# Routed attention with a gated MLP: batch 0 in three rounds of queries, and cluster codes turned several tiles at a time

## The chip, the cores and the metric

The kernel runs on one core of one Trainium2 chip. The metric is the device time of one execution in microseconds. A core has five engines that run their own instruction streams in order and meet only by semaphores: TensorE (PE in the profile, its weight loads PEld), VectorE (DVE), ScalarE (ACT), GpSimd (POOL) and SyncE (SP), which issues most transfers.

## The reference

Four batches of eight heads, 768 positions, 64 features. Each query and each key is assigned to one of 16 centroids of its head; a query attends only to keys of its own cluster. The result, with the heads side by side, goes through an MLP of width 2048 with a SiLU gate.

```python
q_n = q / (np.linalg.norm(q, axis=-1, keepdims=True) + 1e-06)
k_n = k / (np.linalg.norm(k, axis=-1, keepdims=True) + 1e-06)
c_n = centroids / (np.linalg.norm(centroids, axis=-1, keepdims=True) + 1e-06)
q_assign = np.argmax(np.einsum('bhsd,hcd->bhsc', q_n, c_n), axis=-1)
k_assign = np.argmax(np.einsum('bhsd,hcd->bhsc', k_n, c_n), axis=-1)
mask = q_assign[:, :, :, None] == k_assign[:, :, None, :]
scores = np.where(mask, scale * np.matmul(q, k.transpose(0, 1, 3, 2)), -1000000000.0)
attn = np.exp(scores - np.max(scores, axis=-1, keepdims=True))
attn = attn / (np.sum(attn, axis=-1, keepdims=True) + 1e-09)
x = np.matmul(attn, v).transpose(0, 2, 1, 3).reshape(B * S, H * D)
h = x @ w_in
out = (h * (1.0 / (1.0 + np.exp(-h)))) @ w_out
```

## The kernel before

**Tiles.** A sequence of 768 positions is six tiles of 128. Heads are prepared in pairs (p = 0 to 3). Matmuls take float16, and the mask is made part of the scores: the operand tile "ab" holds 64 rows of features and, in rows 64 to 79, a one-hot code of the cluster, scaled so that keys of another cluster are pushed far down before the exponential.

**Preparing a pair** (`part`, from L474). A float32 tile of queries or keys is split into a high float16 half (`hi`, L524 to L531, on ACT, DVE or POOL) and the rest (`lo`, L533 to L535, on DVE), side by side in "hl". Both halves are turned so that features lie on partitions. The logits against the centroids (L615 and L619, or L624) give the cluster; `peak` and `mark` make the one-hot code on DVE.

- Batch 0 turns on TensorE against an identity (L570). It turns each tile twice: first all 128 columns of high and low half into "lt", for the logits (the settle from PSUM is L585 on ACT, L587 on DVE), and after the code is known the 80 columns of high half and code together, into "ab" (settled by L581 on ACT or L583 on DVE, where "gain" scales the code's rows). The lists `TK`, `TQ`, `TR`, `TS` choose the settling engine.
- Batches 1 to 3 turn by a transposing DMA from SP (L550). POOL subtracts the maximum (L673), DVE makes the code (L700, L702) and flips it in blocks of 32 (L715), and four copies of 16 partitions place it in "ab" (L732 on POOL, L728 by a DMA); `PUTB` gives the engine of each, here POOL, POOL, SP, POOL.

**Attention** (from L762). For each head: scores (L801, six key tiles against 256 or 512 query columns), the exponential on ACT (L808, always 512 columns), PV (L829, with a 65th column that sums the row), reciprocal and normalization on DVE (L842, L847). After each pair x is turned into "xt", by TensorE (L877, settled by L882 or L884) or by a transposing DMA (L866).

**Rounds.** Batch 0 runs its heads twice, `ROUNDS = [(0, 2), (2, 6)]`: first with the first two query tiles, then with the other four. Its MLP runs in three units of two tiles (256 columns), the other batches' in two units of three (384 columns).

**MLP** (from L896). For each of 16 blocks of width: four accumulating matmuls (L907), tanh on ACT (L913), the gate on DVE (L918); then the second matrix (L942), an eviction (L955, L957) and a store from SP. Both weights are cast to float16 on their way in by DMAs from POOL (L976, L980), each behind a one-element copy (L974) that holds it back until a chosen exponential is done.

**Order.** Nothing is run in the order in which it is written. Each step gets an engine, a planned duration, its predecessors, its buffers and a key; `Plan.order` (L88) simulates the engines and transfers in Python and always takes the step that can start first, ties by key. The instruction streams are what it puts out. `AT` and `ML` are the keys of attention and MLP; `LEADS`, `REST`, `RLOAD` and `SOON` say how far ahead a preparation is allowed to start, `sizes` how many buffers each tile has, and a filler (L353) puts matmuls of zeros into PE's planned gaps up to a planned time of `UNREAD` ns.

**Start.** The centroids' square sum, root (`c_root` on POOL, L433), reciprocal and split (L436 to L439), one transpose (L446) and four copies (L451 to L458) give "stk".

## Time and profile before

| | |
|---|---|
| three runs | 307.46, 308.21, 309.07 us; median 308.21 |
| profiled execution | 307.14 us on the device, of which the profile's span is 305.3 |
| granted TensorE clock | 0.998 of full speed |
| moved by DMA | 41.82 MB |
| code placements L732, L728 | 72 on POOL, 24 by DMA |
| first up-projection (L907) starts | 34.9 us |

The profile shows one execution. A group's line gives source line, engine, operation, output and input tile, shape and count; then the busy time in us and the mean of one in ns; then the idle time in front of it and what ended it. In a table of stages each row is a stretch of the span with its length, the busy time of each engine, the granted clock, the share of the DMA engines and GB/s. Matmuls are pipelined and their ends are modelled, so the mean of one (219 ns for a transpose) is its passage, not the pace at which they follow each other.

### The profile page before, as it was taken

The page shows a single profiled execution, that of the slowest core. Times are in us where ns is not written, and L with a number is a line of the kernel's source. Part 1 is how long each engine was busy: PE and PEld are TensorE (multiplying, and loading weights), DVE is VectorE, ACT ScalarE, POOL GpSimd, SP SyncE. Part 2 cuts the span into 40 slices and gives each one's busy share as a digit, 9 for nine tenths or more (in the row PEclk, how much of TensorE's full clock was granted, in tenths as well). Part 3 has the DMA queues.
Part 4 walks back from the last instruction along what each step waited for, and adds up shares of the span by engine and source line. Part 5 has one row for each costly group of instructions (what it writes and reads, how often), then busy time and mean ns, then how long its engine had stood idle before and what let it go on. Part 6 is the DMA issues. An engine that isn't in the chain of part 4 may idle for free.

```text
span 305.3 us, 8425 instructions
## 1 busy us (share of the span) xinstructions
PE 297.3 (97%) x3257; PEld 196.1 (64%) x3257; DVE 207.9 (68%) x493; ACT 223.7 (73%) x461; POOL 108.2 (35%) x218
## 2 busy tenths in 40 slices
PE   8999999999999999999999998999999999999995
PEld 6898777577677746666656765665655565554644
DVE  5999688778869955989766997867562323750820
ACT  5869999888988838999777998778782380642721
POOL 2546432656466480717564563733000000000000
PEclk9999999999999999999999999999999999999999
DMA  7999969993969888486969848472010201002001
GB/s 245 290 249 251 206 104 224 103 248 87 226 100 237 191 167 196 138 156 162 237 149 223 155 154 169 131 129 66 0 37 36 84 12 71 35 0 73 32 34 69
DMA packets 73688, 41.82 MB, mean 137 GB/s; under 512 B 53041, under 2 KB 70705, under 8 KB 73649
## 3 DMA queue, kind: packets, MB, share of 16 engines
q1 hardware_dynamic: 68944, 36.94, 51.4%
q0 software_dynamic: 4288, 4.20, 8.6%
q8 instruction: 25, 0.41, 0.6%
q10 hardware_dynamic: 416, 0.16, 0.2%
q14 instruction: 15, 0.11, 0.1%
HBM read 27.30 MB, written 6.29 MB: 110 GB/s over the span
## 4 chain that ended last, share of the span: by engine, by line
PE 80%; DMA 7%; ACT 5%; DVE 3%; issue 1%; POOL 1%; SPq 0%; ACTq 0%; POOLq 0%
PE bank L942 27%; PE bank L907 22%; PE bank L801 16%; PE bank L829 9%; ACT P L808 4%; DMA ab<-hl 3%; PE bank L570 3%; DMA wout_s<-in_moe_w_out_dram 2%; PE bank L624 2%; DMA nk<-in_k_dram 2%; POOL hl L531 1%; PE bank L615 1%; DVE hl L535 1%; DVE gq L918 1%; PE bank L619 1%
## 5 line engine op out<-in xcount | busy, mean ns | idle before, releaser
L808 ACT ACTIVATE P<-bank 128x512 f16<-128x512 f32 x288 | 157.8, 640 | 30.8 <-PE bank L801 29.1
L942 PE MATMUL bank<-wout_s,gq 128*128 128x512 f16 (+1 forms) x400 | 97.1, 370 | 0.4 <-DMA wout_s<-in_moe_w_out_dram 0.4
L907 PE MATMUL bank<-xt,win_s 128*128 128x384 f16 (+1 forms) x576 | 95.6, 308 | 0.0
L918 DVE SCALAR_TENSOR_TENSOR gq<-tn,bank 128x384 f16<-128x384 f32 (+1 forms) x144 | 70.1, 504 | 32.4 <-ACT tn L913 28.7
L801 PE MATMUL bank<-ab 80*128 80x256 f16 (+1 forms) x384 | 90.9, 326 | 0.0
L913 ACT ACTIVATE tn<-bank 128x384 f32<-128x384 f32 (+1 forms) x144 | 67.8, 488 | 24.1 <-PE bank L907 20.9
L907 PEld LDWEIGHTS <-win_s 128*128 128x128 f16 x576 | 55.0, 97 | 28.8
L942 PEld LDWEIGHTS <-gq 128*128 128x128 f16 x400 | 37.9, 98 | 33.1 <-issue 0.7
L829 PEld LDWEIGHTS <-P 128*128 128x128 f16 x1152 | 45.6, 97 | 11.9 <-ACT P L808 0.8
L829 PE MATMUL bank<-vt,P 128*128 128x65 f16 x1152 | 49.8, 193 | 0.7 <-ACT P L808 0.6
L732 POOL COPY ab<-ohT 16x384 f16<-16x384 f16 x72 | 39.3, 546 | 28.2 <-DVE ohT L715 11.7
L801 PEld LDWEIGHTS <-ab 80*128 80x128 f16 x384 | 34.6, 97 | 20.7 <-DVE ab L583 0.2
L673 POOL TENSOR_TENSOR Df<-L,mx 128x192 f32<-128x192 f32 x24 | 12.3, 511 | 41.9 <-DVE mx L661 39.7
L957 DVE COPY ot<-bank 128x512 f32<-128x512 f32 x18 | 12.3, 681 | 16.4 <-PE bank L942 15.6
L535 DVE SCALAR_TENSOR_TENSOR hl<-nk,hl 128x384 f16<-128x384 f32 (+1 forms) x29 | 19.8, 687 | 3.3 <-POOL hl L531 3.1
L535 DVE SCALAR_TENSOR_TENSOR hl<-nq,hl 128x384 f16<-128x384 f32 (+3 forms) x33 | 20.9, 635 | 0.6 <-POOL hl L531 0.3
L641 DVE TENSOR_REDUCE L<-bank 128x192 f32<-128x384 f32 x24 | 13.3, 552 | 10.0 <-PE bank L624 9.7
L847 DVE TENSOR_TENSOR xn<-bank,rz 128x384 f16<-128x384 f32 (+2 forms) x40 | 19.1, 477 | 1.4 <-DVE rz L842 0.2
L531 POOL TENSOR_SCALAR hl<-nk 128x384 f16<-128x384 f32 (+1 forms) x25 | 13.6, 547 | 7.6 <-PE bank L570 6.7
L955 ACT COPY ot<-bank 128x512 f32<-128x512 f32 (+1 forms) x7 | 3.7, 524 | 17.2 <-PE bank L942 17.2
L531 POOL TENSOR_SCALAR hl<-nq 128x384 f16<-128x384 f32 (+2 forms) x27 | 15.2, 566 | 1.7 <-DMA nq<-in_q_dram 1.1
L417 POOL CAST vt<-nv 128x384 f16<-128x384 f32 x26 | 14.6, 582 | 1.1 <-DMA nv<-in_v_dram 0.7
(60 smaller groups left out, 183.6 us busy)
## 6 DMA issues: line engine op xcount, KB each, us to landing
nv<-in_v_dram SPq DMA_DIRECT2D x16, 384.0 KB, 5.6
out_dram<-ot SPq DMA_DIRECT2D x23, 256.0 KB, 2.3
nk<-in_k_dram SPq DMA_DIRECT2D x15, 384.0 KB, 4.3
nq<-in_q_dram SPq DMA_DIRECT2D x12, 384.0 KB, 4.7
wout_s<-in_moe_w_out_dram POOLq DMA_DIRECT2D x8, 256.0 KB, 7.2
win_s<-in_moe_w_in_dram POOLq DMA_DIRECT2D x4, 512.0 KB, 9.3
nq<-in_q_dram SPq DMA_DIRECT2D x4, 256.0 KB, 6.5
nk<-in_k_dram SPq DMA_DIRECT2D x2, 192.0 KB, 2.8
```

Of the source, the lines that this page charges most:

```text
L417: (nc.gpsimd if eng == "POOL" else nc.vector).tensor_copy(dst, src)
L531: nc.gpsimd.tensor_scalar(out=dh, in0=src, scalar1=qs, scalar2=1.0, op0=ALU.mult, op1=ALU.mult)
L535: nc.vector.scalar_tensor_tensor(out=dl, in0=src, scalar=qs, in1=dh, op0=ALU.mult, op1=ALU.subtract)
L732: nc.gpsimd.tensor_copy(dst, src)
L801: nc.tensor.matmul(banks[sb.i][:, at : at + 128 * (c1 - c0)], ab[0:80, kt[j], :], ab[0:80, qt + c0 : qt + c1, :].rearrange("p n c -> p (n ...
L808: nc.scalar.activation(out=T["P"][P.i][:, 0:at], in_=banks[sb.i][:, 0:at], func=AF.Exp, bias=0.0, scale=ESC if b else -ESC)
L829: nc.tensor.matmul(banks[O.i][:, (D + 1) * t : (D + 1) * t + nn], w, vt[:, VW * j : VW * j + nn], start=(j == 0), stop=(j == NJ - 1), skip ...
L847: nc.vector.tensor_tensor(out=T["xn"][xn.i][:, 0:nq, (h % 2) * D : (h % 2) * D + D], in0=banks[O.i][:, 0 : (D + 1) * nq].rearrange("p (t c ...
L907: nc.tensor.matmul(banks[bank.i][:, 0:n], win_s[:, r, ts(fb, 128)], T["xt"][xtb[b].i][:, r, 128 * j0 : 128 * j1], start=(r == 0), stop=(r ...
L913: nc.scalar.activation(out=T["tn"][tn.i][:, 0:n], in_=banks[bank.i][:, 0:n], func=AF.Tanh, bias=0.0, scale=1.0)
L918: nc.vector.scalar_tensor_tensor(out=T["gq"][g.i][:, fb % 4, 0:n], in0=T["tn"][tn.i][:, 0:n], scalar=1.0, in1=banks[bank.i][:, 0:n], op0=A ...
L942: nc.tensor.matmul(banks[bank.i][:, 0 : c1 - c0], T["gq"][gqs[fc // 4].i][:, fc % 4, ts(t, 128)], wout_s[:, fc, c0:c1], start=(fc == 0), s ...
```

## The change

**Rounds.** Batch 0 runs its heads three times, two query tiles each. The remaining queries are prepared in eight parts of four tiles instead of four of eight, and six of these are split wholly on POOL (`both`, in `LO` the letter P).

**Codes in batch 0.** The first turn now settles straight into "ab"; "lt" is gone. The one-hot codes go to a tile of their own, "oh", 32 columns a tile, and one transpose turns one, two or four tiles of codes at once. The pieces of 16 rows are then copied over the low half's rows in "ab" by the engines that the strings in `TQ` and `TS` name: a digit 1 or 2 gives the number of tiles turned together; without one it is four, and A, D, P or S stand for ACT, DVE, POOL or SP; POOL and SP read from an int16 copy that DVE makes.

**Others.** In batches 1 to 3, `PUTB` places the code by POOL, DVE, POOL, DVE. Two heads share a PSUM bank and one normalization where they fit. In units of 256 columns two blocks of the MLP share a bank, a tanh and a gate. The last pair of batches 1 to 3 has x turned by DMA. The centroids are turned by two transposes and placed by one copy. Buffer counts, keys, leads and engine choices are new; so are some durations and two constants in the planner. `UNREAD` goes from 80 to 60 us of planned time.

```diff
-    ROUNDS = [(0, 2), (2, 6)]
+    ROUNDS = [(0, 2), (2, 4), (4, 6)]
...
+    COUNT = [5, 4, 2, 2, 5, 8, 15, 6, 2, 2, 3, 20, 1, 3, 11, 3, 6, 7, 3, 2]
...
-    UNREAD = 80000.0
+    UNREAD = 60000.0
...
-    PUTB = ["POOL", "POOL", "SP", "POOL"]
-    VC = ["ACT", "ACT", "POOL", "ACT"]
+    PUTB = ["POOL", "DVE", "POOL", "DVE"]
+    VC = ["POOL", "ACT", "DVE", "POOL"]
...
-    TK = ["ACT", "ACT", "DVE", "DVE", "DVE"]
-    TQ = ["DVE", "ACT", "DVE", "DVE", "DVE"]
-    TR = ["ACT", "DVE", "DVE", "DVE"]
-    TS = ["ACT", "DVE", "DVE", "DVE"]
-    HI = ["ACT", "ACT", "ACT", "POOL"]
-    HR = ["DVE", "POOL", "DVE", "POOL"]
+    TK = ["DVE", "ACT", "ACT", "DVE", "ACT"]
+    TQ = ["2DA", "DDPP", "APDD", "DAAP", "DDDD"]
+    TR = ["DVE", "DVE", "ACT", "DVE", "ACT", "DVE", "ACT", "ACT"]
+    TS = ["2DD", "2DD", "DDDD", "1DA", "2DA", "2DD", "2AA", "ASDD"]
+    HI = ["ACT", "ACT", "POOL", "POOL"]
+    HR = ["ACT", "DVE", "ACT", "DVE", "DVE", "ACT", "POOL", "ACT"]
+    LO = ["P", "P", "P", "D", "P", "P", "D", "P"]
...
-    SOON = [7, 4, 7, 4]
-    XT = ["DVE", "ACT", "ACT", "DVE"]
+    SOON = [8, 9, 7, 2]
+    XT = ["DVE", "DVE", "DVE", "DVE", "DVE", "DVE", "DVE", "DVE", "DMA", "DVE", "DMA", "DMA"]
+    XL = ["DMA", "DMA", "DMA"]
...
     def c_place():
...
+        nc.vector.tensor_copy(stk.rearrange("p s h c -> p (s h c)"), banks[pc.i].bitcast(f16)[:, 0 : 2 * H * HC])
...
+            def both(views=views, qs=qs, m=m):
+                src, dh, dl = views()
+                x = T["xs"][xs.i][:, 0 : 64 * m].rearrange("p (h j d) -> p h j d", h=src.shape[1], d=D)
+                nc.gpsimd.tensor_scalar(out=x, in0=src, scalar1=qs, scalar2=1.0, op0=ALU.mult, op1=ALU.mult)
+                nc.gpsimd.tensor_copy(dh, x)
+                nc.gpsimd.tensor_tensor(out=dl, in0=x, in1=dh, op=ALU.subtract)
...
-                w = {"ACT": 200 + act_w(32 * n) * 0.75, "POOL": pool_w(32 * n), "DVE": dve_w(32 * n, 0.08, 240), "SP": 600}[code_eng[g]]
+                w = {"ACT": 200 + act_w(32 * n) * 0.75, "POOL": 155 + 32 * n, "DVE": dve_w(32 * n, 0.08, 240), "SP": 600}[code_eng[g]]
...
+                def turn_code(c0=c0, c1=c1, bk=bk):
+                    for i in range(c0, c1, side):
+                        m = min(side, c1 - i)
+                        at = (i - c0) // side * 128
+                        nc.tensor.transpose(
+                            banks[bk.i].bitcast(f16)[0 : 32 * m, at : at + 128],
+                            T["oh"][oh.i][:, i : i + m, :].rearrange("p n c -> p (n c)"), ident,
+                        )
...
+                def settle_code():
+                    nc.vector.tensor_copy(T["oc"][oc.i][:, 0:wide], banks[bank.i].bitcast(i16)[:, 0:wide])
...
+                    def put_alone(c0=c0, c1=c1, bk=bk, on_a=on_a, cols=cols, g=g):
+                        dst = T["ab"][A.i][64 : 64 + HC, a0 + c0 + g : a0 + c1 : side, :]
+                        src = banks[bk.i].bitcast(f16)[32 * g : 32 * g + HC, 0:cols].rearrange("p (n c) -> p n c", c=128)
+                        if on_a:
+                            nc.scalar.activation(out=dst, in_=src, func=AF.Copy, bias=0.0, scale=ONE)
+                        else:
+                            nc.vector.tensor_scalar(out=dst, in0=src, scalar1=ONE, scalar2=None, op0=ALU.mult)
...
+                def put_near(g=g, cols=cols):
+                    dst = T["ab"][A.i][64 : 64 + HC, a0 + g : a0 + n : 4, :]
+                    rows = slice(32 * g, 32 * g + HC)
+                    if near[g] in "PS":
+                        src = T["oc"][oc.i][rows, 0:cols].rearrange("p (n c) -> p n c", c=128)
+                        if near[g] == "P":
+                            nc.gpsimd.tensor_copy(dst, src)
+                        else:
+                            nc.sync.dma_start(dst, src)
...
+        both = 2 if 2 * nq * (D + 1) <= 512 else 1
...
-        for fb in range(NFB):
+        m = 512 // n if n >= 128 and NFB % (512 // n) == 0 and 512 // n <= 2 else 1
+        for fb in range(0, NFB, m):
...
-        return step("POOL", 840, f, after=[x], use=[use], key=-1, load=2450 if kind == "in" else 1220)
+        return step("POOL", 1180, f, after=[x], use=[use], key=-1, load=2390 if kind == "in" else 1190)
```

In `COUNT` the buffers are, in order, nk 5 (4 before), nq 4 (5), nv 2, hl 2 (3), ab 5, vt 8 (10), P 15 (18), gq 6 (7), xt 2 (3), xn 2 (3), L 3 (2), mx 20 (2), Df 1 (2), oh 3 (2), ohT 11 (3), tn 3, ot 6 (2), rz 7 (3), and the new oc 3 and xs 2.

More of the change, by code (lines that the diff above doesn't have):

```diff
@@ L47, in __init__, with step @@
         self.filler = None
-    def step(self, eng, w, fn, after=(), use=(), key=0.0, load=None, hold=0.0, pace=None, flip=False, lag=None, slack=0.0, port=False):
+    def step(self, eng, w, fn, after=(), use=(), key=0.0, load=None, hold=0.0, pace=None, flip=False, lag=None, slack=0.0, port=None):
         s = Step()
@@ L472, with part @@
     score_uses = {}
-    def part(b, p, segs, a0, due, lead=20.0, hi_eng="POOL", turn="DMA", twin=False, sub="POOL", code_eng=None, pace=None, wait=None):
+    def part(b, p, segs, a0, due, lead=20.0, hi_eng="POOL", turn="DMA", twin=False, sub="POOL", code_eng=None, pace=None, wait=None, lo_eng="D"):
         key = due - lead
@@ L576, in settle_of @@
[L576 to L584 removed]
+                            banks[bank.i].bitcast(f16)[:, (t - c0) * 128 : (t - c0) * 128 + 128],
@@ L585, in settle @@
+                            T["hl"][hl.i][:, t * 128 : t * 128 + 128], ident,
+                        )
+                def settle(bank=bank, c0=c0, c1=c1):
+                    pt = banks[bank.i].bitcast(f16)[:, 0 : (c1 - c0) * 128]
+                    out_ = T["ab"][A.i][:, a0 + c0 : a0 + c1, :].rearrange("p n c -> p (n c)")
+                    if turn[0] == "ACT":
                         nc.scalar.copy(out_, pt)
@@ L740, in part @@
         else:
-            last = {}
-            for c in chunks:
-                bank = buf("M")
-                x = step("PE", 57 * len(c), turn_of(c, bank, D, HW), after=[marks, his, s_ident], use=[hl, bank], key=key + 12 * span)
+            near = turn[1]
+            alone = near[0] in "12"
+            bank = buf("M")
+            side = int(near[0]) if alone else 4
+            wide = 128 * ((n + side - 1) // side)
+            cuts = [(c, min(n, c + 8 * side)) for c in range(0, n, 8 * side)] if alone else [(0, n)]
```

439 lines of the change are left out of this document (222 added, 217 removed).

## The prediction

> **What bounds the kernel now.** I read the page's busy line first, then the busy times by stage, then the chain of waits, then the groups by form. The first line says that TensorE (PE) is busy nearly all the time:
>
> ```profile
> PE 297.3 (97%) x3257; PEld 196.1 (64%) x3257; DVE 207.9 (68%) x493; ACT 223.7 (73%) x461; POOL 108.2 (35%) x218
> ```
>
> The stages say where it is not (columns: stage, its length, busy us of PE, weight loads, DVE, ACT, POOL with counts, granted clock, DMA share, GB/s):
>
> ```profile
> 7.60:15.00 7.40, 6.84 (x142) 6.57 (x143) 7.11 (x21) 6.56 (x12) 3.75 (x6) 1.00 1.02 299
> 15.00:20.00 5.00, 5.00 (x105) 4.54 (x103) 4.93 (x15) 4.65 (x10) 2.47 (x5) 1.00 0.97 186
> 20.00:30.00 10.00, 9.26 (x195) 8.37 (x194) 9.61 (x27) 7.80 (x17) 5.64 (x11) 1.00 1.15 278
> 30.00:50.00 20.00, 19.94 (x284) 15.46 (x281) 15.17 (x43) 19.75 (x48) 7.38 (x15) 1.00 0.94 167
> 50.00:80.00 30.00, 29.48 (x379) 20.52 (x376) 24.66 (x65) 26.98 (x60) 15.50 (x31) 1.00 0.85 157
> ...
> 120.00:160.00 40.00, 39.62 (x471) 25.62 (x470) 32.50 (x73) 35.13 (x72) 22.49 (x42) 1.00 0.72 170
> 160.00:210.00 50.00, 49.06 (x567) 31.79 (x566) 39.91 (x94) 43.15 (x87) 26.66 (x50) 1.00 0.72 152
> ```
>
> After 7.6 us PE's visible idle time is 0.56 + 0.74 + 0.06 + 0.52 + 0.38 + 0.94 = 3.2 us. Two regimes are to be seen. From 7.6 to 30 us DVE is 97% busy (21.65 of 22.4): there it sets the pace of the preparation that feeds PE. From 30 us on, MLP work is always waiting and PE itself is the bound. Matmul ends are modelled, so I tested this with the pace at which long runs issue, from the chain:
>
> ```profile
> 13.31 1.79 PE bank L570 x32
> ...
> 131.69 5.33 DMA ab<-hl
> ...
> 183.53 5.20 DMA ab<-hl
> ...
> 270.49 10.36 PE bank L942 x48
> 280.85 10.40 PE bank L907 x64
> 291.25 10.41 PE bank L942 x64
> ```
>
> These give 0.216 us for a 512-column matmul (10.36/48), 0.1625 for 384, 0.056 for a transpose (1.79/32). Times the counts (368 and 32 half ones on L942; 384, and 192 of 256 columns at 0.109, on L907; 192 + 192 on L801; 1152 at 1.09/36 = 0.030 on L829; 222 transposes; 480 logits at 0.025 to 0.03) this is about 290 us. PE's real work starts near 6.8 and ends at 301.7, so at most about 5 us of it is stall. The last 3.6 us are the last eviction and store, which nothing here touches. Thus the time is PE's work, plus about 5, plus two ends; a change pays where it removes PE instructions, or fills the ramp.
>
> **Code transposes (L570, second use).** Each of 96 tiles of batch 0 is turned twice now:
>
> ```profile
> L570 PE MATMUL bank<-ident,hl 128*128 128x128 f16 x96 | 6.9, 219 | 0.0
> L570 PE MATMUL bank<-ident,hl 128*80 128x128 f16 x96 | 6.9, 219 | 0.0
> L353 PE MATMUL bank<-zeros 128*128 128x256 f16 x42 | 6.8, 320 | 1.0 <-DVE zeros L331 1.0
> ```
>
> The second row shrinks to one per one, two or four tiles: from TQ and TS, 4+2+4+4+4 = 18 in the first round instead of 64, and 2+2+1+4+2+2+2+1 = 16 instead of 32 later. That removes 62 x 0.056 = 3.5 us: 2.6 in the ramp, 0.9 after it. The turns of x (L877) go from 30 to 18, since the last pairs of batches 1 to 3 go by DMA: 0.7 us less. The centroids get one more: 0.06. PE in sum: -4.1 us. Scores, PV, logits and MLP keep their columns (96 scores of 256 for 48 of 512: 10.4 us both ways). Of the 42 idle-filling matmuls 35 lie before 7.6 us and cost nothing; the other 7 (0.76 us) stand in waits and go at nothing: without them the waits remain.
>
> **DVE in the ramp** must shrink as much, or PE's 2.6 us only become waiting. Out go four centroid copies (0.88), a memset (0.22), six first settles on L587 and seven second ones on L583, eight recip/norm pairs (0.45 each, 3.62), two x settles (0.56):
>
> ```profile
> L583 DVE TENSOR_SCALAR ab<-bank,gain 80x1024 f16<-80x1024 f16 x10 | 7.3, 741 | 1.2 <-PE bank L570 0.9 <-ACT P L808 0.3
> ...
> L587 DVE COPY lt<-bank 128x1024 f16<-128x1024 f16 x9 | 5.9, 684 | 0.2 <-PE bank L570 0.2
> ...
> L884 DVE COPY xt<-bank 128x512 f16<-128x512 f16 x1 | 0.4, 415 | 0.0
> ```
>
> That is 0.88 + 0.22 + 6 x 0.684 + 7 x 0.741 + 3.62 + 0.56 = 14.6. In come one centroid copy and a memset (0.45), three settles (2.05), ten code pieces of 512 columns at 0.415 and three of 256 at 0.278 (5.0), four merged norms (4 x 0.60 = 2.4), four x settles (1.1), two V casts: no row shows one on DVE; bounds 0.21 (the 96-wide float copy's median) and 0.56 (384 from PSUM), taken 0.35, so 0.7. Sum 11.7: DVE gains 2.9, enough for PE's 2.6. ACT there: out 8.4 (two settles, one code settle 1.14, pair 2's split 1.25, six casts 3.05, two x settles 0.9), in 8.7 (five settles at 1.015, four code pieces near 0.64, two casts): level. POOL takes pair 2's split, V casts and four code pieces, some 5 us on 14 of 30: it has room; without it they would land on DVE.
>
> **Three rounds.** The rest of batch 0's queries come as eight parts of four tiles for four of eight. Six of the eight are split wholly on POOL, three instructions each: 0.416 twice (128x256, one input) and one with two inputs, 0.65 worked out from Df's 511 ns at 192 elements; 1.5 x 6 = 9 us of POOL between 25 and 80 us, where it is about half idle. Bounds: 0 while another unit of MLP work covers PE; 1.5 us once if the first round-two part is late. I take 0. DVE is relieved of about 2.7 there. The paired tanh and gate (24 of 512 columns for 48 of 256) save ACT 18.6 - 24 x 0.64 = 3.2 us and DVE about 1.3. ACT was 99% busy at 30 to 50 us, but PE was dense too, so both are priced at 0; it is cover for the denser second round.
>
> **Codes of batches 1 to 3.** Two of the four placements per part move to DVE, one from POOL, one from an SP transfer:
>
> ```profile
> L732 POOL COPY ab<-ohT x72: 496/500/891, 56.2 to 209.9; 16x384 f16<-16x384 f16 x72
> ...
> L702 DVE TENSOR_SCALAR oh<-Df x24: 198/210/546, 54.2 to 207.6; 128x96 f16<-128x96 f32 x24
> ...
> ab<-ohT SPq DMA_DIRECT2D x24, 12.0 KB, 2.8
> ...
> 53.00:210.00 157.00, 155.16 (x1815) 102.39 (x1814) 124.15 (x295) 132.88 (x275) 85.42 (x160) 1.00 0.78 165
> ```
>
> POOL loses 24 x 0.55 = 13 us, SP 24 issues of 0.6 us, and the 2.8 us landing leaves the path to the scores. DVE gains 48 copies that the trace does not show: at least 0.2 each (L702's shortest), at most 0.35 alone (between 256 and 512 columns of L884) plus a POOL copy waited for, 0.50, so 0.85; I take 0.35, as the nearest in size. That is 17 us on DVE from 53 to 210 us, where it idles 33 (157 - 124.15, last line). Cost to PE: 0, hidden in that idleness; if it runs out, gates and norms come late, tanh waits for banks, then PE. The preparation of a part now starts two heads ahead (SOON's last) instead of four; the chain shows what lateness costs, the two transposing transfers of over 5 us that end in PE waits of 0.38 and 0.94. Two heads of PE work are 17 us (per batch 42 of MLP, 24 of scores and PV, 3 of logits; a quarter of it); one part takes about 10 by its rows (split 0.55 + 0.66, transfer 4.1 to 5.3, the DVE and POOL steps 0.55 + 0.35 + 0.51 + 0.54 + 0.58, logits 0.5, placing 1.1). I price this at 0 and leave it to the range. Loads, weights and stores keep their bytes.
>
> **The root** stays on POOL, as before; only its memsets go. The last DMA turn of x (3.6 us to landing) has behind it batch 2's MLP, which ran 7 us past the last attention before.
>
> **Sum.** Profiled execution 307.14 (305.3 + 1.84 around it), minus 4.1: **303.0 us**. The median shown is 1.07 above that execution; with that offset the same sum is 304.1.
>
> **Rivals.** A: the new order also removes the stalls. For it: the planner's POOL copy is now 155 + 384 = 539 ns against 546 measured (it was 494), its paced weight load 1180 instead of 840 against 0.26 + 0.75 and the gaps. Against: only 3.2 us and 0.76 of filler are there. Time 303.0 - 4.0 = 299.0. B: PE's saving turns into waiting, because 30 to 50 us is ACT's (19.75 of 20) and the ramp's loads fill the DMA (share 1.02 to 1.15); then only the late 1.6 (0.9 + 0.7) counts, 305.5, and with one new wait like the chain's 0.94 it is 306.5. For it: those rows; against: DVE, the ramp's fullest engine, gets lighter. The Trainium skill (Perfetto Trace Analysis, Identifying the Most-Contended Engine) says that PE's headroom is to be judged by weight-load busy share, not matmul busy share; at 64% it would grant PE a third of slack, and the time would stay at 307. The trace disagrees: at 290.9 to 301.4 matmuls follow at full pace with a load of 98 ns in each 216.
>
> C, slower: **DVE's copies and POOL's lock each other out.** Both are released by the same flip (L715), so each DVE copy meets a POOL copy. The spread speaks for it: L702 takes 198 to 546 ns, L732 496 to 891, for one shape each. DVE's fullest stretch was 97% busy, so of 157 us it can use 152: 28 are free, and 1 more from gates. 48 copies overrun that from 29/48 = 0.60 us each, and eat PE's 4.1 too from 33/48 = 0.69. Between that and the bound of 0.85, at 0.77, they are 37 us: 8 over, less 4.1, net +4: 311.0 (315 at the bound). Against: L702's median is 210, so most do not collide. The Trainium skill (SBUF — State Buffer, SBUF: two separate sides) states it as a rule: the two engines' shared port pair is held for a whole instruction and the loser blocks. By that rule alone C would be the forecast; the medians show blocking to be the exception.
>
> **Chances.** Forecast 0.47, A 0.20, B 0.13, C 0.20. The range, 298.5 to 310.0, holds A, B and most of C; the likeliest case's own is 300.5 to 305.5. No change means within 0.5% (306.7 to 309.7 around the median), which is what a measurement here can tell. Faster: 0.45 + 0.20 + half of B 0.06 = 0.71; same: 0.02 + 0.07 + 0.03 = 0.12; slower 0.17.
>
> **What would show it.** L570's second row split: 96 settled turns and some 34 code turns; L877 x18; PE busy near 293. DVE busy at 7.6 to 30 below 97%, first up-projection (L907) before 34.9 us, where it began. The new DVE copies near 0.35 us, DVE under 90% from 80 to 210. PE idle after 7.6 us near 3. I am wrong if PE idle rises above 6 (then the wait in front of L801 or L829 names the culprit), or if the time falls while PE's count does not.

## The result, and the profile after

Twenty executions of the changed kernel have a median of 309.33 us, twenty of the kernel before beside them 307.45: ratio 1.0063, interval [1.0045, 1.0082]. It is slower, by about 1.9 us. The profiled execution has a span of 307.7 us, against 305.3.

The page's busy line of the changed kernel, then its busy times by stage (columns as before: stage, its length, busy us of PE, weight loads, DVE, ACT, POOL with counts, granted clock, DMA share, GB/s):

```profile
PE 300.8 (98%) x3260; PEld 201.1 (65%) x3260; DVE 212.8 (69%) x532; ACT 225.7 (73%) x442; POOL 103.6 (34%) x215
```

```profile
7.60:15.00 7.40, 7.27 (x160) 6.70 (x161) 7.17 (x20) 6.06 (x11) 4.30 (x6) 1.00 0.66 225
15.00:20.00 5.00, 4.27 (x57) 3.40 (x55) 4.64 (x17) 3.50 (x5) 1.72 (x3) 1.00 1.00 314
20.00:30.00 10.00, 9.61 (x148) 7.92 (x148) 6.53 (x23) 9.66 (x19) 8.04 (x18) 0.83 0.74 146
30.00:50.00 20.00, 19.96 (x308) 17.16 (x307) 11.92 (x44) 19.47 (x41) 14.03 (x30) 1.00 1.20 238
50.00:80.00 30.00, 29.88 (x377) 22.49 (x374) 22.94 (x60) 26.00 (x53) 13.16 (x27) 1.00 0.82 187
80.00:210.00 130.00, 129.69 (x1480) 84.90 (x1478) 106.95 (x257) 103.87 (x210) 53.98 (x105) 1.00 0.67 158
...
160.00:210.00 50.00, 50.00 (x522) 30.93 (x520) 39.60 (x99) 39.66 (x79) 18.38 (x36) 1.00 0.46 105
```

PE's visible idle time after 7.6 us is only 0.13 + 0.73 + 0.39 + 0.04 + 0.12 + 0.31 = 1.7 us, less than the 3.2 before, and the late waits at 160 to 210 us are gone. Yet the kernel is slower. The groups by form say why the busy row misleads:

```profile
L360 PE MATMUL bank<-zeros 128*128 128x256 f16 x70 | 11.9, 320 | 1.0 <-DVE zeros L340 1.0
...
L577 PE MATMUL bank<-ident,hl 128*128 128x128 f16 x96 | 7.7, 223 | 0.2
...
L933 PE MATMUL bank<-ident,xn 128*128 128x128 f16 x18 | 2.6, 227 | 0.0
L734 PE MATMUL bank<-ident,oh 128*64 128x128 f16 x14 | 1.9, 229 | 0.0
L734 PE MATMUL bank<-ident,oh 128*128 128x128 f16 x16 | 1.8, 244 | 0.3 <-DVE oh L671 0.3
L734 PE MATMUL bank<-ident,oh 128*32 128x128 f16 x4 | 0.4, 222 | 0.0
```

The removed work is removed: 96 + 34 transposes for 192, 18 turns of x for 30. But there are 70 matmuls of zeros for 42, and 40 of them lie after 7.6 us, where 7 did. At 0.109 us each they fill 4.4 us of planned waiting (0.8 before): idle time that the busy row counts as work.

So I leave the zeros out and count what PE still has to do. Each matmul of the trace is taken at the pace worked out in the prediction (0.216 us for 512 columns, 0.056 for a transpose, and so on), and the sum of those not yet issued is the work left, in us (two of the experiments below stand beside):

```
at us          5     20     30     40     50     80    200
before     288.7  276.9  268.4  258.4  248.7  219.6  101.2
after      284.7  276.0  268.8  261.4  251.8  222.6  103.3
b_turn     286.0  276.2  268.1  258.2  248.4  220.7  101.4
re_plan2   285.0  275.1  267.4  258.2  253.0  227.3  109.6
```

The changed kernel starts with 4.0 us less. At 30 us it is 0.4 behind, at 40 us 3.0; later it regains 0.9. **The whole loss, 7.0 us, lies before 40 us:** 3.1 of it from 5 to 20 us, 1.3 from 20 to 30 and 2.6 from 30 to 40.

What is late there is the MLP, which fills PE beside the attention. The line of the up-projections, after (durations, then first and last start):

```profile
L966 PE MATMUL bank<-xt,win_s x576: 269/325/328, 42.5 to 292.0; 128*128 128x384 f16 x128, 128*128 128x256 f16 x64
```

They begin at 42.5 us, 7.6 later than before. They need x of all four pairs of batch 0's first round, and the fourth pair's is copied into place after (start, duration, count at the end):

```profile
37.92 0.28 DVE L940 COPY xt<-bank 128x256 f16<-128x256 f16 x1
```

and before:

```profile
34.58 0.28 DVE L884 COPY xt<-bank 128x256 f16<-128x256 f16 x1
```

Before 38.2 us, then, no MLP work could fill PE's waits, where the kernel before had some from 34.9 on; 17 of the zeros stand in this time, from 32.9 us on. From 38.2 to 42.5 PE is busy with attention and preparations, which the order puts first.

The weights start late as well. GpSimd's timeline, after (brackets: idle time in front and what ended it):

```profile
18.02 0.61 POOL L783 COPY ab<-oc 16x512 f16<-16x512 f16 x1 [4.89 <-DVE oc L751]
...
20.06 0.84 POOL L783 COPY ab<-oc 16x256 f16<-16x256 f16 x2 [0.19 <-DVE oc L751]
...
21.43 0.40 POOL L542 TENSOR_SCALAR xs<-nq 128x256 f32<-128x256 f32 x1
21.90 0.53 POOL L543 CAST hl<-xs 128x256 f16<-128x256 f32 x1
22.51 0.67 POOL L544 TENSOR_TENSOR hl<-xs,hl 128x256 f16<-128x256 f32 x1
23.12 0.19 POOL L1032 CAST pace<-P 128x1 f32<-128x1 f16 x1
23.25 0.95 POOL L1038 DMA_DIRECT2D wout_s<-in_moe_w_out_dram  x1
...
25.18 0.76 POOL L1034 DMA_DIRECT2D win_s<-in_moe_w_in_dram  x1
```

and before:

```profile
7.28 0.97 POOL L974 CAST pace<-hl 128x1 f32<-128x1 f16 x1 [2.80 <-ACT hl L527]
8.19 0.95 POOL L980 DMA_DIRECT2D wout_s<-in_moe_w_out_dram  x1
...
14.01 0.81 POOL L976 DMA_DIRECT2D win_s<-in_moe_w_in_dram  x1
```

The first weight leaves at 23.25 us, where it left at 8.19. That is the order's doing more than GpSimd's: the list `PW` ties each weight to a step of another engine, the first one before to ScalarE's split that ends at 7.2 us (L527), the first one after to an exponential. Followed from the list into the trace, that exponential ends at 22.19 us, and the weight leaves 1.06 us behind it; with GpSimd idle the kernel before took 0.59 (20.00 to 20.59). The code pieces that wait 4.89 us for DVE and the split of 1.60 us stand in front of the weight and cost it about half a microsecond. What the late start does to the transfers is in the stages, after:

```profile
0.00:15.00 15.00, 13.64 (x200) 11.36 (x201) 11.26 (x35) 9.60 (x16) 5.89 (x22) 1.00 0.71 226
15.00:20.00 5.00, 4.27 (x57) 3.40 (x55) 4.64 (x17) 3.50 (x5) 1.72 (x3) 1.00 1.00 314
20.00:25.00 5.00, 4.63 (x66) 3.63 (x66) 2.50 (x10) 4.97 (x11) 4.68 (x10) 0.80 0.37 125
25.00:30.00 5.00, 4.98 (x84) 4.29 (x83) 4.03 (x14) 4.70 (x10) 3.36 (x9) 0.86 1.11 167
30.00:40.00 10.00, 10.00 (x152) 8.34 (x151) 6.66 (x24) 9.53 (x20) 8.01 (x18) 1.00 1.23 206
```

and before:

```profile
0.00:15.00 15.00, 13.31 (x194) 11.57 (x195) 11.57 (x39) 10.52 (x18) 5.92 (x26) 1.00 0.89 271
15.00:20.00 5.00, 5.00 (x105) 4.54 (x103) 4.93 (x15) 4.65 (x10) 2.47 (x5) 1.00 0.97 186
20.00:25.00 5.00, 4.37 (x91) 4.00 (x90) 4.75 (x13) 2.80 (x8) 1.37 (x4) 1.00 1.12 307
25.00:30.00 5.00, 4.89 (x108) 4.37 (x106) 4.86 (x15) 5.00 (x11) 4.27 (x8) 1.00 1.18 250
```

At 20 to 25 us the DMA engines are 37% busy where they were 112%. Length times GB/s gives 6.42 MB by 30 us, before 7.78: 1.36 MB behind, which is 6.6 us at the 206 GB/s of the next stage. But nothing in this trace waits for it. The quarter of win_s that the first up-projections read is issued at 28.57 us and lands at 36.04, ahead of the fourth pair's x; none of PE's waits is put down to a weight; and from 20 to 43 us neither PE nor DVE, ScalarE or GpSimd shows a wait that ends with a transfer. That the late weights cost the changed kernel anything is not shown.

The clock is 0.80 and 0.86 from 20 to 30 us: 5 x 0.20 + 5 x 0.14 = 1.7 us of PE lost. And ScalarE stops its exponentials between 15.3 and 20.6 us; by 20 us it has started 3 of them, in the kernel before 11:

```profile
13.63 1.67 ACT L855 ACTIVATE P<-bank 128x512 f16<-128x512 f32 x3
...
18.36 0.59 ACT L788 ACTIVATE ab<-bank 16x512 f16<-16x512 f16 x1 [0.94 <-DVE ab L791]
18.97 1.01 ACT L586 COPY ab<-bank 128x1024 f16<-128x1024 f16 x1
20.01 0.58 ACT L788 ACTIVATE ab<-bank 16x512 f16<-16x512 f16 x1
20.62 2.56 ACT L855 ACTIVATE P<-bank 128x512 f16<-128x512 f32 x5
```

That is the settling and code placing of the other pairs. The wait of 0.94 us is for DVE, which reads the same PSUM bank. The next scores, head 4's, start at 18.38 us, when pair 2's codes come into place, behind 11 zeros from 17.14 on; their exponentials then stand behind a settle and a piece of pair 1 in ScalarE's own stream. Head 1's codes are complete only at 20.90, on GpSimd (the row at 20.06 above); in the kernel before its exponentials began at 15.5. DVE, which all these codes pass through, is busy 4.64 of the 5 us from 15 to 20.

### The profile page after: what moved, and what is told of

It is laid out like the page before. It is cut to its first block, busy times and chain, and to the rows that moved or that the text cites. A ratio compares the mean times of both kernels' runs of the same rounds, so it can differ in the third digit from the quotient of the medians.

```text
span 307.7 us, 8357 instructions
## 1 busy us (share of the span) xinstructions
PE 300.8 (98%) x3260; PEld 201.1 (65%) x3260; DVE 212.8 (69%) x532; ACT 225.7 (73%) x442; POOL 103.6 (34%) x215
## 4 chain that ended last, share of the span: by engine, by line
PE 88%; DVE 6%; issue 2%; POOL 1%; DMA 1%; ACT 1%; DVEq 0%; ACTq 0%
PE bank L1000 26%; PE bank L966 25%; PE bank L848 19%; PE bank L879 11%; PE bank L360 2%; PE bank L613 2%; DVE hl L548 2%; DMA ab<-oc 1%; DVE gq L977 1%; PE bank L734 1%; PE bank L577 1%; DVE oc L751 0%; DVE mx L645 0%; DVE ab L712 0%; DVE ab L791 0%
## 5 line engine op out<-in xcount | busy, mean ns | idle before, releaser
L855 ACT ACTIVATE P<-bank 128x512 f16<-128x512 f32 x288 | 151.9, 626 | 24.9 <-PE bank L848 22.0
L848 PE MATMUL bank<-ab 80*128 80x256 f16 (+1 forms) x432 | 87.6, 309 | 0.9 <-DVE ab L712 0.3
L972 ACT ACTIVATE tn<-bank 128x384 f32<-128x384 f32 (+1 forms) x120 | 61.1, 537 | 28.1 <-PE bank L966 27.1
L848 PEld LDWEIGHTS <-ab 80*128 80x128 f16 x432 | 38.0, 97 | 21.9 <-issue 1.4
L710 POOL COPY ab<-ohT 16x384 f16<-16x384 f16 x48 | 24.2, 504 | 34.0 <-DVE ohT L694 23.2
L424 POOL CAST vt<-nv 128x384 f16<-128x384 f32 x28 | 15.4, 558 | 27.2 <-PE bank L879 23.6
L712 DVE COPY ab<-ohT 16x384 f16<-16x384 f16 x48 | 18.4, 383 | 1.1
L905 DVE TENSOR_TENSOR xn<-bank,rz 128x384 f16<-128x384 f32 (+1 forms) x36 | 18.3, 509 | 1.1 <-PE bank L933 0.3
L548 DVE SCALAR_TENSOR_TENSOR hl<-nq,hl 128x384 f16<-128x384 f32 (+2 forms) x31 | 18.2, 588 | 0.0
L1013 ACT COPY ot<-bank 128x512 f32<-128x512 f32 x8 | 4.7, 586 | 18.4 <-PE bank L1000 18.4
L1015 DVE COPY ot<-bank 128x512 f32<-128x512 f32 (+1 forms) x17 | 10.9, 653 | 8.0 <-PE bank L1000 7.8
## 6 DMA issues: line engine op xcount, KB each, us to landing
out_dram<-ot SPq DMA_DIRECT2D x23, 256.0 KB, 2.2
wout_s<-in_moe_w_out_dram POOLq DMA_DIRECT2D x8, 256.0 KB, 8.4
nq<-in_q_dram SPq DMA_DIRECT2D x4, 256.0 KB, 4.8
```

The costliest lines, as they stand in the source:

```text
L424: (nc.gpsimd if eng == "POOL" else nc.vector).tensor_copy(dst, src)
L548: nc.vector.scalar_tensor_tensor(out=dl, in0=src, scalar=qs, in1=dh, op0=ALU.mult, op1=ALU.subtract)
L710: nc.gpsimd.tensor_copy(dst, src)
L712: nc.vector.tensor_copy(dst, src)
L848: nc.tensor.matmul(banks[sb.i][:, at : at + 128 * (c1 - c0)], ab[0:80, kt[j], :], ab[0:80, qt + c0 : qt + c1, :].rearrange("p n c -> p (n ...
L855: nc.scalar.activation(out=T["P"][P.i][:, 0:at], in_=banks[sb.i][:, 0:at], func=AF.Exp, bias=0.0, scale=ESC if b else -ESC)
```

## The experiments

The theory to test: the ramp up to 40 us takes back what PE saves, because late weights, the chains through ScalarE and DVE, or a slow clock pace it. Rivals: DVE and GpSimd lock each other out later (case C of the prediction); a single wait; the fillers. "In its own order" means that the planner's order is kept and only what a step issues is changed.

**a_fill**: zeros planned at 14 to 18 us twice, against the slow clock.

```diff
     for s in plan.order():
         s.fn()
+        if s.eng == "PE" and s.key == 1e9 and 14000 < s.start < 18000:
+            s.fn()
```

> The changed kernel in its own order, with each of the 14 filler matmuls that its plan puts between 14 and 18 us issued twice (14 more of 0.11 us). Theory clock: TensorE ran at half speed from 22.98 to 26.39 us because it had too little to do at 15 to 20 us; with more filler the granted clock stays 1.0 from 20 to 30 us, the 3.4 us at half speed give back about 1.2 to 1.7 us, and the span falls from 307.7 to about 306.3. Rival: TensorE was waiting for codes and exponentials there anyway; the clock may stay whole, but the span stays at 307.7, or grows by up to 0.6 where the filler stands in front of the scores.

308.29 us, ratio 1.0016 [0.9992, 1.0039], clock 1.0. The slow stretch is gone, and by the medians of the ratios 0.47%, 1.4 us, with it. Two kernels that carry the same edit, a_lean and a_codes below, came out at 1.0049 and 1.0032 with clock 1.0; if their other edits cost nothing, the clock's share is between 0.4 and 1.4 us. That it is not all is plain.

**a_bank**: pair 2's codes turned into a second bank too, from which ScalarE reads.

```diff
-                        nc.tensor.transpose(
-                            banks[bk.i].bitcast(f16)[0 : 32 * m, at : at + 128],
...
+                        for other in (bk.i, 2) if near == "DAAP" else (bk.i,):
+                            nc.tensor.transpose(
+                                banks[other].bitcast(f16)[0 : 32 * m, at : at + 128],
...
-                        src = banks[bank.i].bitcast(f16)[rows, 0:cols].rearrange("p (n c) -> p n c", c=128)
+                        src = banks[2 if near == "DAAP" else bank.i].bitcast(f16)[rows, 0:cols].rearrange("p (n c) -> p n c", c=128)
```

> The changed kernel in its own order; the one-hot codes of pair 2 are transposed a second time into a free PSUM bank (4 more transposes, 0.22 us), and ScalarE reads its two pieces from there, VectorE its own from the first bank. Theory bank: pieces of one bank taken by two engines run one after the other, as ScalarE's idle 0.94 us in front of its second piece (18.36 us) shows; with two banks that wait is gone, the fourth exponential starts at about 20.0 instead of 20.6 us, and the span falls by 0.4 to 0.7 us. Rival: VectorE's and ScalarE's own work sets that stretch; the fourth exponential moves by less than 0.2 us and the span by nothing.

308.52 us, ratio 1.0032 [1.0008, 1.0055]. The clock was 1.0 here too, and ScalarE's pieces of these codes were partly zeros, since fillers write that bank. So two things changed, and **a_both** tried again, with the fillers sent to bank 4 and doubled:

> The changed kernel in its own order, with the idle-filling matmuls planned at 14 to 18 us issued twice (as in a_fill), and pair 2's code transposes written to a second bank as well, which ScalarE's pieces read, so that DVE and ScalarE no longer take turns at one bank (three more transposes of 0.056 us and an empty second bank; nothing is left out). Theory 1 (the order itself costs most, and the time above it is the half-speed stretch and the shared bank): the bank's wait of 0.94 us goes on top of a_fill's gain, so about 0.9 us below a_fill's ratio of 1.0016: ratio 0.997 to 1.000. Rival (the shared bank is off the path; what a_bank gained was the clock alone): as a_fill, ratio 1.0016, within 0.001.

310.06 us, ratio 1.0075 [1.0047, 1.0103]. Neither theory: the doubled fillers stood 2.4 us long in front of the scores of 18 us, and ScalarE idled 0.4 us at 20 to 22.5 instead. What the shared bank costs stays open.

**b_put**: in the kernel before, the four placements of codes of batches 1 to 3 by POOL, DVE, POOL, DVE, in its own order.

```diff
-                    if code_eng[g] == "SP":
-                        nc.sync.dma_start(dst, src)
-                    elif code_eng[g] == "ACT":
-                        nc.scalar.copy(dst, src)
-                    elif code_eng[g] == "POOL":
+                    if g % 2 == 0:
                         nc.gpsimd.tensor_copy(dst, src)
                     else:
```

> The kernel before in its own order, only that the codes of batches 1 to 3 are placed by POOL, DVE, POOL, DVE instead of POOL, POOL, SP, POOL. Case C of the prediction (the two engines lock each other out): DVE gains 48 x 0.77 = 37 us and the time grows by 2 to 4 us. The prediction's own price: DVE gains some 18 us in its idleness, POOL loses 13 us, the time stays within 0.5 us, or falls by up to 1 where a late code made PE wait (the waits of 0.38 and 0.94 us).

316.05 us, ratio 1.0276 [1.024, 1.0312]: a slowdown of case C's size and more. Its groups show that it isn't case C:

```profile
L728 POOL COPY ab<-ohT 16x384 f16<-16x384 f16 x48 | 25.9, 539 | 37.3 <-DVE ohT L715 15.4 <-PE bank L797 12.5 <-PE bank L903 3.8
...
L730 DVE COPY ab<-ohT 16x384 f16<-16x384 f16 x48 | 17.2, 357 | 1.4
```

and its PE waits (in total, times, longest):

```profile
PE bank L624 <- DMA ab<-hl: 3.8, 4, 1.8
PE bank L903 <- DVE gq L914: 1.4, 2, 0.8
PE bank L938 <- DVE gq L914: 1.3, 3, 0.8
```

DVE's copy takes 357 ns, and 48 of them wait 1.4 us in all. GpSimd's, moved from SP's place in the order, stands 15.4 us waiting for DVE's flip, and a split queued behind it reaches the transposing transfer late (3.8 us of PE, 1.3 before). Moved without re-planning, a copy costs by what stands behind it. In the changed kernel, planned for it, the copies take:

```profile
L710 POOL COPY ab<-ohT 16x384 f16<-16x384 f16 x48 | 24.2, 504 | 34.0 <-DVE ohT L694 23.2 <-issue 4.3 <-PE bank L966 2.7
...
L712 DVE COPY ab<-ohT 16x384 f16<-16x384 f16 x48 | 18.4, 383 | 1.1
```

The mean hides two kinds. In the trace 21 of the 48 DVE copies take 0.25 to 0.27 us; the other 27 take 0.36 to 0.56, and each of these ends 0.11 to 0.12 us after a GpSimd instruction that had begun before it. So the lock of case C is there; it costs a copy 0.1 to 0.3 us, and DVE has room for that.

**b_nofill**: the kernel before without its 7 fillers after 7.6 us.

```diff
     for s in plan.order():
+        if s.eng == "PE" and s.key == 1e9 and s.start > 7500:
+            continue
         s.fn()
```

> The kernel before in its own order, without the 7 filler matmuls that come after 7.6 us. The prediction priced them at nothing: the time stays at about 307.5. Theory clock: they keep TensorE's clock up through the first preparations; without them a stretch at half speed appears between 10 and 30 us and the time grows by 1 to 2 us.

306.91 us, ratio 0.9973 [0.9944, 1.0003]: they cost nothing that can be told, and no slow stretch appears without them. **a_lean** asked the same of the zeros after 20 us in the changed kernel, 17 of them at 32.9 to 37.9:

```diff
+        idle = s.eng == "PE" and s.key == 1e9
+        if idle and s.start > 20000:
+            continue
         s.fn()
+        if idle and 14000 < s.start < 18000:
+            s.fn()
```

> The changed kernel in its own order, with a_fill's doubled fillers, but without the idle-filling matmuls planned later than 20 us (17 of them stand between 32.9 and 37.9 us, some 2 us of PE). Theory 1 (they stand in waits for ScalarE's exponentials and for pair 3's codes, since no MLP work is ready there before 42 us): time as a_fill, ratio 1.0016 within 0.002. Rival (PE has real work by then and the fillers only take its time): 2 us less than a_fill, ratio 0.995.

308.81 us, ratio 1.0049 [1.0018, 1.0080]: above a_fill by more than the 0.002 allowed, and in any case no gain, so they stand in waits. With them gone the stages show the real idle time:

```profile
30.00:35.00 5.00, 4.29 (x65) 3.29 (x62) 2.19 (x9) 5.00 (x12) 4.63 (x10) 1.00 1.23 197
35.00:40.00 5.00, 4.40 (x72) 3.62 (x72) 3.78 (x15) 4.94 (x11) 3.10 (x8) 1.00 1.22 225
```

ScalarE is full (9.94 of 10) and the DMA over 1.2; PE waits 1.3 us. What PE waits for in these 10 us is neither, but the code pieces that DVE places, 1.1 of the 1.3 (in total, times, longest):

```profile
PE bank L848 <- DVE ab L766: 1.1, 2, 0.6
```

**b_turn** tests the step of the prediction itself, in the order of the kernel before: every second code transpose is left out.

```diff
                     for i, t in enumerate(c):
+                        if c1 == HW and i % 2:
+                            continue
                         nc.tensor.transpose(
...
```

> The kernel before in its own order, with every second code transpose of batch 0 left out (48 of 96: 32 of the first round, 16 of the second); the settle writes each turned tile twice, so its own cost stays, and the second tile of each two gets its neighbour's codes and values. Step of the prediction (a removed transpose is worth its 0.056 us in the ramp as after it): 48 x 0.056 = 2.7 us less, ratio 0.991. Rival (in the ramp PE is not the bound, so that only the 16 later ones count): 0.9 us less, ratio 0.997. Rival 2 (the second round's are in the ramp too, at 20 to 40 us where ScalarE is full): no gain, ratio 1.000.

306.20 us, ratio 0.9946 [0.9917, 0.9976]: 1.7 us of the 2.7, between the step and its first rival, though its profiled execution (305.4 span) shows none. Its stages in the ramp:

```profile
15.00:20.00 5.00, 4.26 (x88) 3.63 (x87) 4.97 (x13) 4.47 (x10) 3.38 (x6) 1.00 0.98 183
20.00:30.00 10.00, 9.25 (x179) 8.11 (x177) 9.76 (x29) 8.51 (x18) 6.04 (x11) 1.00 1.15 286
```

At 15 to 20 us PE now idles 0.74 (0 before) while DVE is 99% busy. In the table above 2.7 us less work at 5 us has become 0.2 less at 40. The runs and this one trace differ: by the interval 0.7 to 2.6 us are gained, so the step is not refuted by b_turn, only its trace shows where such a saving can turn into waiting.

**a_act** and **a_dve** ask which engine sets the pace after 23 us: three exponentials, or four of DVE's normalizations, are issued twice on top of a_fill.

```diff
+        if s.fn.__name__ == "exp" and s.start > 23000 and twice < 3:
+            s.fn()
+            twice += 1
```

> The changed kernel in its own order with a_fill's doubled fillers, and three exponentials of ScalarE between about 25 and 30 us issued twice (nothing is left out; 3 x 0.65 us of ScalarE more). Theory 1 (ScalarE sets the pace from 20 to 42 us, so what TensorE saves before that only becomes waiting): all of it shows, 1.6 to 2.0 us above a_fill's ratio of 1.0016, so 1.007 to 1.008. Rival (PE sets the pace there as it does later): ratio 1.002, within 0.002.

> The control for a_act: the same kernel with four normalisations of DVE (L905, 0.43 us each, 1.7 us in all) between about 24 and 34 us issued twice, ScalarE's as they are. Theory 1: DVE is 45 to 80% busy there and not the bound; ratio as a_fill, 1.0016 within 0.002. Rival (DVE sets the pace of the ramp, as the prediction had it up to 30 us): 1.7 us more, ratio 1.007.

310.56 us, ratio 1.0106 [1.0069, 1.0143], and 310.30, ratio 1.0077 [1.0047, 1.0107]. Both show, in full or more (about 2.8 us above a_fill for 1.95 added, 1.9 for 1.7), though DVE has room there in the changed kernel (4.03 of 5 us at 25 to 30, 6.66 of 10 at 30 to 40). Their PE work left at 45 us is 1.4 and 1.6 above a_fill's (257.4 and 257.6 against 256.0). So theory 1 fails for DVE, and it is no single engine: the chain runs through both, and this order has no slack for either at these places.

**a_codes**: a_fill with ScalarE's three code pieces of pairs 1 and 2 placed by DVE.

```diff
-                    elif near[g] == "A":
+                    elif near[g] == "A" and n < 16:
```

> The changed kernel in its own order with a_fill's doubled fillers; the three code pieces of pairs 1 and 2 that ScalarE places in the first round (0.59 us each, 16 to 20 us) are placed by DVE at the same points of the order (0.42 us each). Nothing is left out. Theory 1 (ScalarE paces the ramp, and taking turns with DVE at one bank costs it up to 0.94 us more): 1 to 2 us less than a_fill, ratio 0.995 to 0.999. Rival (at 12 to 20 us DVE is the one that is full, 95% busy, and gets 1.3 us more): 1 us more than a_fill, ratio 1.005.

309.13 us, ratio 1.0032 [1.0008, 1.0055]: nearer to the rival. Its PE work left at 40 us is 261.5, a_fill's 260.6. Relieving ScalarE at DVE's cost gains nothing.

**b_late**: the kernel before with the changed kernel's list of what releases the weights; its planner orders anew.

```diff
-    PW = [11, 5, 7, 13, 12, 27, 17, 2, 21, 10, 14, 19]
+    PW = [13, 8, 17, 13, 8, 32, 25, 17, 16, 13, 12, 7]
```

> The kernel before with one list of its planner changed, PW, to the values of the changed kernel: the exponentials that release the twelve weight transfers. The order around them is planned anew by its own planner; nothing else is changed and nothing is left out. First weights go out at about 17 us instead of 8, win_s at 18 to 32 instead of 14 to 27. Theory 1 (by 30 us the changed kernel has moved 1.36 MB less, and weights that start late cost the ramp): 1 to 3 us above the kernel before, ratio 1.003 to 1.010, with the first up-projection later than 34.9 us or PE waiting for weights. Rival (weights have slack; their lateness in the changed kernel follows from something else): ratio 1.000 within 0.002.

310.54 us, ratio 1.0076 [1.0041, 1.011]. Its PE waits:

```profile
PE bank L801 <- DMA ab<-ohT: 1.7, 1, 1.7
PE bank L907 <- DMA win_s<-in_moe_w_in_dram: 1.3, 1, 1.3
```

By 45 us it is 1.7 us behind the kernel before (255.1 left against 253.4), with PE waiting for win_s; another 1.9 is lost around 110 us to a late code, a matter of the new order. So late weights can cost 1.7 us in an order in which the fourth pair's x is in place at 34.9 us. In the changed kernel that x comes 3.3 us later, behind the weight it meets, so b_late does not price the weights there. The changed kernel with its weights released early was not run.

**re_plan to re_plan4**: can another order keep the 4.1 us? In re_plan the planner knows that two engines don't read one bank at a time and takes 1.65 us for GpSimd's split; buffer counts, priorities and engines are chosen anew.

```diff
+                    for b in s.use:
+                        if b.i is not None and b.pool in self.psum and b in self.seen:
+                            for en, tt in self.seen[b].items():
+                                if en != s.eng:
+                                    t = max(t, tt)
...
-                his.append(step("POOL", 3 * pool_w(64 * m), both, after=lds, use=[nat, hl, xs], key=key, pace=pace))
+                his.append(step("POOL", 1650, both, after=lds, use=[nat, hl, xs], key=key, pace=pace))
...
```

> The changed kernel with the same instructions to choose from but another order: its planner now knows that two engines do not read one PSUM bank at a time and that a split wholly on GpSimd takes 1.65 us, not 1.1; buffer counts, priorities and the engines of the small copies are chosen anew under these. Nothing is left out. PE's counts stay near the changed kernel's. Theory 1 (the saving of 4.1 us on PE is real, and the order of the ramp and what it got wrong spent it): the first up-projection begins before 38 us, and the time falls below the kernel before, ratio 0.985 to 0.996. Rival (the ramp can't be fed faster by any order with these parts): as the changed kernel, ratio 1.003 to 1.006.

316.17 us, ratio 1.0223 [1.0159, 1.0287]. At 30 us it has kept 1.4 us of its lead (267.0 left, before 268.4; at 5 us it was 3.7), then one wait ends it:

```profile
PE bank L592 <- POOL hl L559: 4.5, 1, 4.5
```

The split waited 5.9 us for a load of queries that took 9.6 us to land among three weights, and the clock fell behind the wait (0.79 at 30 to 40 us). **re_plan2** moves that one load forward in SP's stream:

> re_plan with one step moved: the load of pair 2's later queries is issued one place earlier on SP, right behind pair 1's, not behind a turn of x that made it wait 5.5 us and then share the DMA with three weight transfers (9.6 us to landing; 4.5 us of PE waiting behind it, then half speed). Theory 1 (this one late load and the slow clock behind it cost 4.5 us and about 3.5 us: 10 us at 0.79 and 20 us at 0.93): 308 us, ratio 0.996 to 1.003. Rival (there are more such places in an order that has not been tried): above ratio 1.008.

316.58 us, ratio 1.0300 [1.0261, 1.034]. At 45 us it is level with the kernel before (253.5 us left against 253.4; the 252.8 in the next expectation is too low by 0.7). Then:

```profile
PE bank L981 <- DMA win_s<-in_moe_w_in_dram: 5.9, 1, 5.9
```

**re_plan3** issues that weight earlier, ahead of six others:

> re_plan2 with one more step moved: the transfer of the last quarter of win_s, behind which PE waited 5.9 us from 45 us, is issued on GpSimd right behind the quarter before it, ahead of six transfers of wout_s. Nothing is left out. At 45 us re_plan2 had 252.8 us of PE work left (the kernel before 253.4, the changed one 256.7). Theory 1 (the 4.1 us can be had, and late weights and loads in the ramp decide whether they are): the wait and the half speed behind it (5 us at 0.78 and 10 us at 0.77, some 3.4 us) go; 316.6 - 9.3 = 307.3 us, ratio 0.996 to 1.002. Rival (the transfers only change places, and the next one is as late): above 1.008.

315.54 us, ratio 1.0241 [1.0201, 1.028]. At 50 us it is 0.2 ahead (248.5 against 248.7), and waits for the next:

```profile
PE bank L1015 <- DMA wout_s<-in_moe_w_out_dram: 4.5, 1, 4.5
```

**re_plan4** sends wout_s in the order of its use, the last four together:

> re_plan3 with the eight transfers of wout_s issued on GpSimd in the order in which the down-projection needs them, the last four together (in re_plan3 the second quarter-kilobyte rows that PE needs came last, and PE waited 4.5 us for them from about 50 us, then ran at half speed). Nothing is left out. At 50 us re_plan3 had 248.2 us of PE work left, the kernel before 248.7, the changed kernel 251.8. Theory 1 (the order of the transfers in the ramp decides): the wait of 4.5 us and 10 us at 0.72 and 10 at 0.94 (3.4 us) go, 315.5 - 7.9 = 307.6 us, ratio 0.994 to 1.001. Rival (the ramp's transfers are too many for 50 us in whatever order, and the wait moves once more): above 1.008.

315.35 us, ratio 1.0241 [1.0213, 1.0269]. The wait is back at the split, since GpSimd now stands in front of it:

```profile
POOL wout_s L1149 <- DMA win_s<-in_moe_w_in_dram: 5.2, 3, 1.9
```

In re_plan neither side held (1.0223 lies above both); in the three that followed the rival did, three times: one long wait was replaced by the next, each 4.4 to 5.9 us. But the saving was spent before them. In re_plan2 and re_plan3, which reach 40 us without a long wait, the lead of 3.7 us at 5 us is 1.8 at 20, 1.0 at 30 and 0.2 at 40: as in the trace of b_turn, what PE saves in the ramp turns into waiting. These orders have moved 4.88 MB (re_plan4) by 25 us; the kernel before 6.53. None beats either kernel. That no order can keep the saving isn't shown.

## Why the prediction was wrong

**The step that failed** is the one on DVE in the ramp: "enough for PE's 2.6". PE's work fell by the 4.1 foretold (4.0 in the trace), and DVE's from 7.6 to 30 us by 3.3 (7.17 + 4.64 + 6.53 = 18.34, before 21.65; 2.9 foretold). But the conclusion, that PE then finishes earlier, doesn't follow. I compared busy sums; what sets the time up to 40 us is when codes, exponentials and x arrive. With it fell "From 30 us on, MLP work is always waiting": in the changed kernel there was none to run before 38.2 us. The ramp took 7.0 us where I had priced 0. The measured time lies inside the range I gave only because that range held the slower rival C too; the direction was wrong.

What the runs showed in its place, row by row: 3.1 us went before 20 us, where settles and code pieces on DVE, ScalarE and GpSimd held the exponentials back from 15.3 to 20.6; 1.3 from 20 to 30, where the clock stood at half for 3.4 us; 2.6 from 30 to 40, where the fourth pair's x was 3.3 us later than before and zeros filled the waits for DVE's code pieces (a_lean). Time added to ScalarE or to DVE after 23 us shows in full (a_act, a_dve), and the clock's part by runs is 0.4 to 1.4. That the code pieces are the cause of the first part is read from the trace and not tested: a_codes moved three of them and a_both unshared a bank, and neither brought the time down.

**What I didn't price.** I wrote that POOL "has room" by busy time, and that weights "keep their bytes". Both are true and neither was the question: the weights left 15 us later, since the new order ties them to later exponentials, and were 1.36 MB behind at 30 us. In another order such a delay cost 1.7 us by 45 us (b_late); in the changed kernel no wait shows for it.

**Fillers.** "Go at nothing" was right, twice (b_nofill, a_lean). But I had taken PE's visible idle time as the sign to watch. It fell to 1.7 us while the zeros after 7.6 us rose to 4.4; the stall was 6.1.

**Terms that held.** ACT level: 33.74 us busy from 7.6 to 45, before 33.75. The new DVE copies: 0.383 us against 0.35, which is luck: I took a copy that meets nobody, and such a one takes 0.25, while 27 of 48 were held up by GpSimd. DVE is 82% busy at 80 to 210 us (106.95 of 130), so rival C's lock came true and its price of 0.77 did not. The prediction called blocking the exception; the trace has it in more than half of the copies. The rule drawn on there, the Trainium skill's on the shared port (SBUF — State Buffer, SBUF: two separate sides), that the loser blocks for the whole instruction, agrees with these 27. The split on POOL: 1.60 us against 1.5. Two heads of lead were enough: PE is 50.00 of 50 at 160 to 210, so the late half of rival A came true, 1.3 us.

**The rivals.** B was nearest: PE's saving turns into waiting. Of its two reasons ScalarE is full there (a_lean), but PE's waits name DVE's codes, and none names a transfer. Its time, 306.5, was too low since it let the ramp absorb the 2.6 us but not lengthen. Its companion rule in the Trainium skill (Perfetto Trace Analysis, Identifying the Most-Contended Engine), to judge PE by weight-load share, still fails at full pace (65% in a kernel with PE dense from 80 us on). But my use of it missed that in the ramp even "PE 10.00 of 10" held 17 matmuls of zeros.

## What to carry to other kernels

Before a saving on the fullest engine is counted, ask in each stage what its next input waits for, and count the work left at several times as well as the busy sums. Late transfers are a cause only where a wait ends with one. Work put into an in-order stream delays what stands behind it, whatever the engine's busy share (b_put, re_plan4). Where idle time is filled with dummy work, subtract it first. And a plan that ends earlier on paper says little about an order that leans on transfers landing on time: re_plan's own plan ends at 299.7 us, the changed kernel's at 301.5.

## What the runs showed of the hardware

- The clock was granted at half for 3.4 us from 23.0 us (0.60 on average from 22.5 to 25 us and 0.86 from 25 to 30) although PE reads 4.27 of 5 us busy at 15 to 20 us. From 17.5 to 20 us there are 18 matmuls in 2.5 us (PE 2.10 busy). The Trainium skill (TensorE: Matmul & The Clock Gate, What's actually happening) has the half rate follow an idle window of about 3.4 us. The stretch at half rate is as long as such a window, but what made a window count as idle no row shows: a_bank has 21 matmuls there, reads only 1.89 busy and kept the full clock.
- Of the changed kernel's 48 DVE copies of 16x384, 21 took 0.25 to 0.27 us. The 27 that took 0.36 to 0.56 all ended 0.11 to 0.12 us after a GpSimd instruction that had begun before them.
- Pieces of one PSUM bank, read by ScalarE and DVE, ran one after the other: ScalarE waited 0.94 us for DVE's. Whether the bank or the program's semaphores ask for that, no run tells.
- GpSimd in re_plan4, with its weights sent close together, waited three times up to 1.9 us for an earlier weight to land before it issued the next. Whether the queue or the program asks for that, no run tells.
